# Window attention and four-expert attention on one core: stage 2 operands as two fp16 parts under a bound per batch, stage 1 softmax of four tiles at once inside PSUM

## The chip, the cores and the metric

The kernel runs on one core of one Trainium2 chip. The metric is the device time of one execution in microseconds, lower is better. The core has TensorE (PE in the rows, with its weight loads as PEld), VectorE (DVE), ScalarE (ACT), GpSimd (POOL), and SyncE (SP), which issues all the DMAs here.

## The reference

```
q, k, v: (8 batches, 8 heads, 576 positions, 64), fp32
# stage 1: sliding-window attention per head; row r sees columns r-63 .. r
scores = 0.125 * q @ k.T;  mask = (0 <= row - column < 64)
x = softmax(where(mask, scores, -1e9)) @ v        # heads side by side: x is (8, 576, 512)
# stage 2: four causal attentions ("experts") over x, the best two of them per position
logits = x @ w_gate (512, 4);  w = softmax over the top 2 of 4
for e in range(4):
    q, k, v = x @ wq[e], x @ wk[e], x @ wv[e]     # 512 -> 64
    ye = softmax(causal(0.125 * q @ k.T)) @ v @ wo[e]
    out += (weight of e in the top 2, else 0) * ye
```

wq and wk are drawn eight times larger than the other weights, so the scores of stage 2 spread widely, and operands that are rounded once are too coarse. That is why products are made of a high and a low part.

## The kernel before, in words

**Stage 1.** Two heads share a pair tile (128 partitions). One tile of work is 64 query rows of both heads against 128 key columns, the older 64 (`old`) and the block's own 64 (`own`). Four tiles are a group, so there are 72 groups `g`, nine per batch. Unit `m` (`s1_mm`, line 311) makes the scores of two groups in two PSUM banks. Unit `q` (`s1_qk`) makes the softmax: one masked minimum per tile on DVE (line 328, a custom instruction whose accumulated result is read by a second one), for groups from `FIRST` = 18 on a DVE minimum that folds the two halves into 64 columns (line 336), four exponentials on ACT, each with a read of its accumulated sum (line 339), and on POOL the division by the sum, four instructions per group (line 353). Unit `t` (`s1_t`) transposes on PE (line 376) and unfolds with masked products on DVE (line 390). Unit `a` (`s1_av`) multiplies by v (line 403) and writes x as high and low fp32r parts, `XH` on ACT (line 412) and `XL` on DVE (line 414).

**Stage 2**, for a batch `b` and a pair of experts `pr` (16 such pairs in all). Units `v` (`s2_v`) project v and the gate's logits; the product is split into three bf16 parts on ACT (line 520), DVE (line 524) and POOL (lines 527 and 528). Units `k` and `r` (`s2_k`, `s2_q`) project keys and queries into two fp32r parts, ACT for the high one and DVE for the low one; the first 64 keys and queries also go into plain fp32 tiles `KF` and `QF`. Unit `x` (`s2_mm`) makes the scores: 30 matmuls at line 625 and one fp32 product of the first block at line 628. Unit `y` (`s2_soft`) masks on DVE (line 640) and takes exponentials on ACT (line 644). Unit `u` (`s2_w`) multiplies by gate over sum and splits into two fp16 parts, the high one on ACT (line 690), the low one on POOL (lines 695 and 696) or, where `LOW` has a D and in the last three pairs, on DVE (line 693). Unit `D` transposes them by DMA (line 704). Unit `A` (`s2_av`, line 727) multiplies v by them, one pass for each entry of `PRODUCTS`; unit `o` (`s2_o`) projects with wo, ACT copies the result, and SP sends it out.

**Order.** Every unit is a generator of steps. A long string `ORDER`, written out in the file, lists the steps; each word runs one step, and a number after a colon names the PSUM banks that the unit takes (there are eight). All five engines run their instructions in the order in which the steps issue them, with semaphores between them.

## Time and profile before

| | us |
|---|---|
| median of 3 runs | 466.24 (465.84 to 468.89) |
| the profiled execution | 467.63 |
| its span, first to last instruction | 465.9 |
| busy: PE 438.8, DVE 376.6, ACT 357.2, POOL 347.3 | |

The profiled execution is 1.4 us above the median, and 1.7 us of it lie outside the span. Busy time of an engine is the union of its instructions' times. An instruction's own duration holds some time in which the next one already runs, so the spacing of starts in a run of equal instructions is the better price of one more of them.

### The profile page before, as it was taken

The numbers are of one execution on the slowest core, as the hardware profiler recorded it, in microseconds if no ns is written. First come the engines' busy times: TensorE is split into PE (matmuls) and PEld (weight loads), VectorE is DVE, ScalarE is ACT, GpSimd is POOL, SyncE is SP. The second block draws the span as 40 slices with busy tenths as digits, with TensorE's granted clock in tenths as the row PEclk, the third lists the DMA queues.
The fourth block names the chain that finished last, engine by engine and source line by source line (L and its number), as shares of the span: only waits on it lengthen the run. The fifth ranks groups of instructions, "written<-read, shape, count | busy, mean of one in ns | idle before, by whom it ended". The sixth has DMA issues, their size and how long they took to land.

```text
span 465.9 us, 17032 instructions
## 1 busy us (share of the span) xinstructions
PE 438.8 (94%) x6192; PEld 388.9 (83%) x6192; DVE 376.6 (81%) x1588; ACT 357.2 (77%) x1304; POOL 347.3 (75%) x865
## 2 busy tenths in 40 slices
PE   7898999999999999999998999999999999999955
PEld 7687899888788887888887988988898898989745
...
GB/s 261 339 275 45 36 257 220 87 156 236 98 272 229 153 171 214 129 167 215 165 163 219 201 161 182 210 136 161 245 136 168 159 146 87 134 115 183 199 183 113
DMA packets 142788, 81.86 MB, mean 176 GB/s; under 512 B 124656, under 2 KB 125680, under 8 KB 142704
## 3 DMA queue, kind: packets, MB, share of 16 engines
...
q14 instruction: 35, 0.29, 0.2%
q10 hardware_dynamic: 80, 0.13, 0.1%
...
## 4 chain that ended last, share of the span: by engine, by line
PE 21%; DVE 9%; ACT 8%; POOL 7%; DMA 4%; issue 3%; SPq 0%; DVEq 0%; POOLq 0%; ACTq 0%
PE ps L727 4%; PE ps L503 4%; DMA tu<-sp 4%; PE ps L504 3%; PE ps L505 3%; PE ps L625 3%; ACT sp L690 3%; ACT p L339 2%; PE ps L403 2%; ACT p L644 2%; POOL sp L696 2%; POOL p L353 1%; DVE sm L328 1%; DVE pt L390 1%; DVE p L336 1%
## 5 line engine op out<-in xcount | busy, mean ns | idle before, releaser
L644 ACT ACTIVATE p<-p,r 128x576 f32<-128x576 f32 (+3 forms) x128 | 77.3, 606 | 23.7 <-DVE r L640 12.1
L339 ACT ACTIVATE p<-p,st 128x64 f32<-128x64 f32 x216 | 72.3, 338 | 22.1 <-DVE p L336 21.8
L696 POOL TENSOR_TENSOR sp<-p,sp 128x320 f16<-128x320 f32 (+3 forms) x91 | 80.7, 886 | 7.6
L690 ACT ACTIVATE sp<-p,r 128x192 f16<-128x192 f32 (+3 forms) x128 | 73.1, 607 | 11.7 <-DMA tu<-sp 7.0
L390 DVE TENSOR_TENSOR pt<-ps,tri 64x512 f32<-64x512 f32 (+1 forms) x120 | 75.8, 633 | 5.0 <-PE ps L376 2.9
L353 POOL TENSOR_SCALAR p<-p,st 128x64 f32<-128x64 f32 x216 | 67.6, 336 | 5.4 <-DVE st L349 4.5
L640 DVE CUSTOM_DVE_ANT_0 p<-ps,causal 128x320 f32<-128x320 f32 (+3 forms) x160 | 68.2, 471 | 3.7 <-POOL sp L696 2.2
L727 PE MATMUL ps<-tu,v 128*64 128x64 f16 (+2 forms) x1760 | 62.1, 229 | 5.3 <-DMA tu<-sp 4.8
L727 PEld LDWEIGHTS <-v 128*64 128x64 bf16 x1760 | 59.0, 112 | 8.9 <-issue 6.7
L328 DVE CUSTOM_DVE_ANT_0 sm<-ps,win 128x128 f32<-128x128 f32 x264 | 62.3, 282 | 4.1 <-PE ps L311 3.6
L695 POOL TENSOR_SCALAR p<-p,r 128x320 f32<-128x320 f32 (+3 forms) x91 | 53.6, 589 | 5.1 <-ACT sp L690 4.2
L625 PE MATMUL ps<-kt,qt 64*128 64x320 f32 (+2 forms) x480 | 50.5, 328 | 3.1 <-DVE vr L524 1.2
L625 PEld LDWEIGHTS ps<-kt,qt 64*128 64x128 f32 x480 | 36.1, 185 | 12.6 <-DVE vr L524 1.6
L311 PE MATMUL ps<-k,q 64*64 64x128 f32 (+1 forms) x1080 | 41.4, 281 | 2.3 <-DMA k<-in_kT_dram 1.8
L403 PE MATMUL ps<-pt,v 128*64 128x64 f32 x1080 | 38.6, 225 | 3.0 <-DMA v<-in_vW_dram 1.1
L339 ACT ACTIVATION_READ_ACCUMULATOR p<-p,st 128x1 f32 x216 | 40.9, 189 | 0.0
L403 PEld LDWEIGHTS ps<-pt,v 128*64 128x64 f32 x1080 | 34.3, 138 | 6.8 <-issue 2.0
L503 PE MATMUL ps<-xh,wqhi 128*128 128x256 f32 (+1 forms) x128 | 39.4, 308 | 0.5 <-DVE vr L524 0.4
L503 PE MATMUL ps<-wvhi,xh 128*128 128x260 f32 x128 | 37.3, 292 | 2.7 <-DVE pt L390 1.9
L503 PE MATMUL ps<-xh,wkhi 128*128 128x256 f32 (+1 forms) x128 | 39.5, 309 | 0.3 <-DVE vr L524 0.2
L311 PEld LDWEIGHTS ps<-k,q 64*64 64x64 f32 x1080 | 32.0, 138 | 8.4 <-issue 3.5
L505 PE MATMUL ps<-xh,wqlo 128*128 128x256 f32 (+1 forms) x128 | 37.8, 296 | 0.0
...
## 6 DMA issues: line engine op xcount, KB each, us to landing
...
tu<-sp SPq DMA_TRANSPOSE x96, 3.7
...
```

The costliest lines, as they stand in the source:

```text
L311: nc.tensor.matmul(S1[g][i][o:o + 64, c:], lhsT=q_t[r, 64 * b:64 * b + 64], rhs=k_t[r, 64 * b + c:64 * b + 128], start=True, stop=True)
L339: nc.scalar.activation(pt[:, i], pt[:, i], AF.Exp, bias=st[:, 0, z + i:z + i + 1], scale=-1.0, accum_out=st[:, 1, z + i:z + i + 1])
L353: nc.gpsimd.tensor_scalar(p, p, st[:, 2, i:i + 1], 1.0, op0=OP.mult, op1=OP.mult)
L390: nc.vector.tensor_mul(t[64 * w:64 * w + 64, :n, e], ps[r, :n], tri[r, w, None, :].to_broadcast([64, n, 128]))
L403: nc.tensor.matmul(o[64 * h:64 * h + 64, 4 * x + i], lhsT=pairs[p][2][:, h, b], rhs=t[:, i, c:c + 64], start=True, stop=True)
L503: nc.tensor.matmul(ps, lhsT=ah, rhs=bh, start=first, stop=False)
L625: nc.tensor.matmul(ps[e][:, at(i):at(i) + n], lhsT=QT[pr][r, w, q], rhs=KT[b, pr][r, m, key:key + n], start=x == 0, stop=x == 2)
L640: nc.vector.tensor_tensor_reduce(out=dst, in0=src, in1=mask, scale=1.0, scalar=3.0e38, op0=OP.add, op1=OP.min, accum_out=to)
L644: nc.scalar.activation(p, p, AF.Exp, bias=r2[:, 0, x:x + 1], scale=-1.0, accum_out=r2[:, 1, x:x + 1])
L690: nc.scalar.activation(hi, p, AF.Copy, scale=by)
L696: nc.gpsimd.tensor_tensor(lo, p, hi, op=OP.subtract)
L727: nc.tensor.matmul(to, lhsT=V2[b % 2][:, c, a, 2 * pr + h], rhs=rhs, start=n == 0, stop=n == len(work_list) - 1, skip_group_check=True)
```

## The change

Stage 1, groups from 18 on: the scores stay in PSUM, one bank per group. One `copy_predicated` of four tiles overwrites, inside the bank, those of the `own` columns that lie in the future by the `old` ones, which leaves 64 columns per tile. Then one DVE reduction gives the four maxima. In four of nine groups (`BY_TILE`) four exponentials follow on ACT from PSUM with their sums, after POOL has scaled the maxima; in the other five DVE subtracts the maxima, ACT takes one exponential of all 256 columns, and DVE sums them. The division on POOL is one instruction per group. Where the older half doesn't exist (the first block of a head pair), a memset fills it.

Stage 2: `s1_av` also takes the largest magnitude of what it writes (`MX`). `s2_top` and `s2_scale` make three bounds per batch from it, with a matmul against the largest weights, and their reciprocals. Values, keys and queries leave PSUM multiplied by these, as two fp16 parts each. The scores are then 16-bit matmuls, the product of the first block is six 64x64 matmuls in place of the fp32 one, the product of the second block has 192 key columns in place of 256, the mask step multiplies by the product of two bounds, and `PRODUCTS` has three entries in place of five. The output copy multiplies by v's bound. All second parts are made on POOL except in the last three pairs.

`ORDER` is written anew. The diff, without it:

```diff
+FAR = 1.0e30
-LOW = "PPPPPPPDP"
+LOW = "PPPPPPPPP"
+BY_TILE = "010101010"
...
+        if i < 3:
+            nc.vector.tensor_reduce(largest[:, i:i + 1], raw, axis=AX.X, op=OP.max, apply_absolute_value=True)
+            nc.gpsimd.memset(bound[:, i], abs(scale) * 4.01 * 2.0 ** -14)
+            nc.gpsimd.tensor_scalar(bound[:, i], bound[:, i], largest[:, i:i + 1], 1.0, op0=OP.mult, op1=OP.mult)
...
     def s1_mm(gs):
+
         ps = [bank().rearrange("r (t c) -> r t c", c=128) for x in range(2)]
         for y, g in enumerate(gs):
-            S1[g] = [ps[i % 2][:, 2 * y + i // 2] for i in range(4)]
-            for i, p, b in tiles(g):
+            S1[g] = [ps[y][:, i] if len(gs) > 1 else ps[i % 2][:, i // 2] for i in range(4)]
+        for i in range(4):
+            for g in gs:
+                p, b = list(tiles(g))[i][1:]
                 c = 64 if i in alone(g) else 0
                 q_t, k_t, _ = pairs[p]
                 for h in range(2):
                     r = slice(64 * h, 64 * h + 64)
-                    o = 64 * (h ^ i % 2)
+                    o = 64 * (h ^ turn(g, i))
                     nc.tensor.matmul(S1[g][i][o:o + 64, c:], lhsT=q_t[r, 64 * b:64 * b + 64],
                                      rhs=k_t[r, 64 * b + c:64 * b + 128], start=True, stop=True)
+
+    def turn(g, i):
+        return i % 2 if g < SOLO else g % 2
...
+            old, own = (bass.AP(ps[0].tensor, ps[0].offset + 64 * x, [ps[0].ap[0], [128, 4], [1, 64]]) for x in range(2))
+            for i in lone:
+                nc.vector.memset(ps[i][:, 0:64], NEG)
+            nc.vector.copy_predicated(own, past[:, None].to_broadcast([128, 4, 64]), old)
+            yield
+            st = sums()
+            top = st[:, 0, z:z + 4]
+            if BY_TILE[g % 9] == "1":
+                nc.vector.tensor_reduce(top, own, axis=AX.X, op=OP.max, negate=True)
                 yield
-        yield
-        if g >= FIRST:
-            for x0, x1 in ((0, lone[0]), (lone[0] + 1, 4)) if lone else ((0, 4),):
-                if x0 < x1:
-                    nc.vector.tensor_tensor(pt[:, x0:x1], sm[:, x0:x1, 0], sm[:, x0:x1, 1], op=OP.min)
-            yield
-        for i in range(4):
-            nc.scalar.activation(pt[:, i], pt[:, i], AF.Exp, bias=st[:, 0, z + i:z + i + 1], scale=-1.0,
-                                 accum_out=st[:, 1, z + i:z + i + 1])
-            if i % 2:
+                nc.gpsimd.tensor_scalar(st[:, 0, z:z + 4], st[:, 0, z:z + 4], 0.125, 1.0, op0=OP.mult, op1=OP.mult)
                 yield
-        P1[g] = pt
+                pt = P1[g] = work.tile([128, 4, 64], F32, tag="p1", bufs=4, name=f"p1_{g}")
+                for i in range(4):
+                    nc.scalar.activation(pt[:, i], ps[i][:, 64:128], AF.Exp, bias=st[:, 0, z + i:z + i + 1],
+                                         scale=0.125, accum_out=st[:, 1, z + i:z + i + 1])
+                    if i % 2:
+                        yield
+                yield from normalize(g, st, z)
+                return
+            nc.vector.tensor_reduce(top, own, axis=AX.X, op=OP.max)
+            yield
+            pt = P1[g] = work.tile([128, 4, 64], F32, tag="p1", bufs=4, name=f"p1_{g}")
+            nc.vector.tensor_tensor(pt, own, top[:, :, None].to_broadcast([128, 4, 64]), op=OP.subtract)
+            yield
+            nc.scalar.activation(pt, pt, AF.Exp, scale=0.125)
+            yield
+            nc.vector.tensor_reduce(st[:, 1, z:z + 4], pt, axis=AX.X, op=OP.add)
+            yield
+        yield from normalize(g, st, z)
...
-        for i in range(n):
-            p = P1[g - (n - 1 - i) // 4][:, i % 4]
-            nc.gpsimd.tensor_scalar(p, p, st[:, 2, i:i + 1], 1.0, op0=OP.mult, op1=OP.mult)
-            if i % 4 == 3:
-                yield
+        for x in range(0, n, 4):
+            p = P1[g - 1 + x // 4 if n == 8 else g]
+            if g < FIRST:
+                for i in range(4):
+                    nc.gpsimd.tensor_scalar(p[:, i], p[:, i], st[:, 2, i:i + 1], 1.0, op0=OP.mult, op1=OP.mult)
+            else:
+                nc.gpsimd.tensor_tensor(p, p, st[:, 2, x:x + 4, None].to_broadcast([128, 4, 64]), op=OP.mult)
+            yield
...
+        if b9 not in MX:
+            MX[b9] = work.tile([128, 5], F32, tag="mx", name=f"mx_{b9}")
+        nc.vector.tensor_reduce(MX[b9][:, k // 2:k // 2 + 1], src, axis=AX.X, op=OP.max, apply_absolute_value=True)
+        yield
...
+    def s2_top(b):
+        mx, MX[b] = MX[b], work.tile([128, 1], F32, tag="top", name=f"top_{b}")
+        nc.vector.tensor_reduce(MX[b], mx, axis=AX.X, op=OP.max)
+
+    def s2_scale(b):
+        ps = bank()[:, :3]
+        top = MX.pop(b)
+        for i in range(3):
+            nc.tensor.matmul(ps[:, i:i + 1], lhsT=bound[:, i], rhs=top, start=True, stop=True)
+        yield
+
+        sc = SC[b] = work.tile([128, 7], F32, tag="sc", bufs=3, name=f"sc_{b}")
+        nc.vector.tensor_tensor(sc[:, 0:3], ps, floor, op=OP.max)
+        nc.vector.reciprocal(sc[:, 3:6], sc[:, 0:3])
+        yield
+        nc.gpsimd.tensor_tensor(sc[:, 6:7], sc[:, 1:2], sc[:, 2:3], op=OP.mult)
+        yield
+        if b % 2:
+            SC4[b] = work.tile([128, 1], F32, tag="sc4", name=f"sc4_{b}")
+            for i in range(2):
+                r = slice(64 * i, 64 * i + 64)
+                nc.gpsimd.tensor_copy(SC4[b][r], SC[b - 1 + i][r, 0:1])
...
-            dst = [V2[(b + i) % 2][at, j, a].rearrange("r e c -> r (e c)") for a in range(3)]
-            rest = work.tile([128, 256], F32, tag="vr", bufs=2, name=f"vr_{b}_{j}_{i}")[at]
-            nc.scalar.activation(dst[0], ps[r, :256], AF.Copy)
+            hi, lo = (V2[(b + i) % 2][at, j, a].rearrange("r e c -> r (e c)") for a in range(2))
+            by = SC[b + i][r, 3:4]
+            nc.scalar.activation(hi, ps[r, :256], AF.Copy, scale=by)
             yield
             if i == 0:
                 nc.vector.tensor_copy(L[b % 2][:, j], ps[:, 256:260])
-            nc.vector.tensor_sub(rest, ps[r, :256], dst[0])
-            yield
-            engine = nc.vector if b == NB - 1 else nc.gpsimd
-            engine.tensor_scalar(dst[1], rest, 1.0, 1.0, op0=OP.mult, op1=OP.mult)
-            engine.tensor_tensor(dst[2], rest, dst[1], op=OP.subtract)
-            if j == 4:
-                yield
+            nc.vector.scalar_tensor_tensor(lo, ps[r, :256], by, hi, op0=OP.mult, op1=OP.subtract)
...
+    def parts(ps, t, by):
+        nc.scalar.activation(t[:, 0], ps, AF.Copy, scale=by)
+        yield
+        nc.vector.scalar_tensor_tensor(t[:, 1], ps, by, t[:, 0], op0=OP.mult, op1=OP.subtract)
...
-    SCORES = (((1, 0, 256), (2, 0, 320)), ((3, 0, 448),), ((4, 0, 320),), ((4, 320, 256),))
+        yield from parts(ps, QT[pr][:, :, c0:c0 + n], SC[b][:, 5:6])
...
-            q = slice(128 * i - 128, 128 * i)
+            q = slice(128 * i - 64, 128 * i + 64)
...
-            nc.tensor.matmul(ps[0][:, 448:512], lhsT=QF[pr].rearrange("r a c -> r (a c)"), rhs=KF[b, pr],
-                             start=True, stop=True)
+            for x, (w, m) in enumerate(((0, 0), (0, 1), (1, 0))):
+                for e in range(2):
+                    r = slice(64 * e, 64 * e + 64)
+                    nc.tensor.matmul(ps[0][r, 448:512], lhsT=QT[pr][r, w, 0:64], rhs=KT[b, pr][r, m, 0:64],
+                                     start=x == 0, stop=x == 2)
...
+        def least(src, dst, mask, to, above=3.0e38):
+            nc.vector.tensor_tensor_reduce(out=dst, in0=src, in1=mask, scale=SC[b][:, 6:7], scalar=above,
...
-    PRODUCTS = ((0, 0), (1, 0), (2, 0), (0, 1), (1, 1))
+    PRODUCTS = ((0, 0), (1, 0), (0, 1))
...
-            copy(t[:, c], ps, h if ends else OUTS[j])
+            by = SC[b][:, 0:1] if j < 4 else SC4[b]
+            if h:
+                nc.vector.tensor_scalar(t[:, c], ps, by, None, op0=OP.mult)
+            else:
+                nc.scalar.activation(t[:, c], ps, AF.Copy, scale=by)
```

Three places show what it does to the engines' queues. VectorE, batch 4, groups 42 and 43 of stage 1 (`sm`, `p` and `st` with their numbers are the tiles of scores, exponentials and sums; `mx` holds the magnitudes for the bounds). Before:

```order
L328 ISA sm_43_3660,st_42_3631<-ps,win 128x128
L328 ISA st_42_3631 128x1
L328 ISA sm_43_3660,st_42_3631<-ps,win 128x128
L328 ISA st_42_3631 128x1
L328 ISA sm_42_3632,st_42_3631<-ps,win 128x128
L328 ISA st_42_3631 128x1
L328 ISA p_42_3633,st_42_3631<-ps,win 128x64
L328 ISA st_42_3631 128x1
L349 RECIPROCAL st_40_3386<-st_40_3386 128x8
L677 RECIPROCAL r_2_1_3363<-r_2_1_3363 128x7
L336 TENSOR_TENSOR p_42_3633<-sm_42_3632 128x192
L328 ISA sm_43_3660,st_42_3631<-ps,win 128x128
```

and in the changed kernel:

```order
L392 TENSOR_REDUCE st_42_3304<-ps 128x4
L375 COPY_PREDICATED ps<-win,ps 128x4x64
L751 RECIPROCAL r_2_0_2746<-r_2_0_2746 128x2
L395 TENSOR_TENSOR p_42_3308<-ps,st_42_3304 128x256
L751 RECIPROCAL r_2_1_3177<-r_2_1_3177 128x7
L477 TENSOR_REDUCE mx_3316<-ps 128x1
L638 TENSOR_REDUCE gs_4_3288<-gt_4_3287 128x1
L814 TENSOR_TENSOR yl_89<-ps,yh_87 128x64
L380 TENSOR_REDUCE st_42_3304<-ps 128x4
```

The per-tile rows of a group (ISA) and the fold are gone; whole-group reductions, a subtraction and the maximum of `s1_av` stand in their place.

TensorE where batch 4's stage 2 begins, the first product of v (`wvhi` by `xh`). Before:

```order
L505 MATMUL ps<-xh_3864,wklo 128x320
L503 MATMUL ps<-xh_3864,wkhi 128x320
L504 MATMUL ps<-xl_3865,wkhi 128x320
L505 MATMUL ps<-xh_3864,wklo 128x320
L503 MATMUL ps<-wvhi,xh_3864 128x260
L504 MATMUL ps<-wvlo,xh_3864 128x260
```

and in the changed kernel, with the bound's three matmuls (`bound` by `top`) ahead of it:

```order
L339 MATMUL ps<-k_3880,q_3879 64x128 x14
L339 MATMUL ps<-k_3917,q_3916 64x64 x2
L579 MATMUL ps<-top_4122,bound 128x1 x3
L567 MATMUL ps<-wvhi,xh_3314 128x260
L568 MATMUL ps<-wvlo,xh_3314 128x260
L569 MATMUL ps<-wvhi,xl_3315 128x260
```

What stood behind a product of the keys stands behind scores of stage 1 and behind the bound, which reads `top` of the same batch.

GpSimd around group 40 and 41's division (`p_40`, `p_41`), same batch. Before:

```order
L527 TENSOR_SCALAR v_1_91<-vr_0_0_3622 128x256
L528 TENSOR_TENSOR v_1_91<-vr_0_0_3622,v_1_91 128x256
L353 TENSOR_SCALAR p_40_3388<-p_40_3388,st_40_3386 128x64 x4
L496 MEMSET sp_72 128x4x64
L679 TENSOR_TENSOR r_2_1_3363<-r_2_1_3363,g_0_89 128x7
L353 TENSOR_SCALAR p_41_3392<-p_41_3392,st_40_3386 128x64 x4
L695 TENSOR_SCALAR px<-px,r_2_1_3363 128x64
L696 TENSOR_TENSOR sp_71<-px,sp_71 128x64
```

and in the changed kernel, around groups 38 and 39:

```order
L773 TENSOR_SCALAR p_1_69<-p_1_69,r_2_0_2746 128x448
L774 TENSOR_TENSOR sp_72<-p_1_69,sp_72 128x448
L417 TENSOR_TENSOR p_38_2910<-p_38_2910,st_38_2872 128x256
L749 TENSOR_SCALAR r_2_0_2746<-r_2_0_2746 128x2
L417 TENSOR_TENSOR p_39_2942<-p_39_2942,st_38_2872 128x256
L586 TENSOR_TENSOR sc_3120<-sc_3120 128x1
L623 TENSOR_TENSOR g_2_4_3240<-g_2_4_3240,below 128x16
```

The split of v (lines 527 and 528) has left this queue, the division is one instruction per group, and a product of bounds (`sc`) has come in.

## Rows read from the trace of the kernel before

**Rows 1.** The page: span, then busy time of each engine.
```profile
span 465.9 us, 17032 instructions
PE 438.8 (94%) x6192; PEld 388.9 (83%) x6192; DVE 376.6 (81%) x1588; ACT 357.2 (77%) x1304; POOL 347.3 (75%) x865
```

**Rows 2.** Windows: stretch, its length, busy us of PE, PEld, DVE, ACT, POOL, clock, DMA.
```profile
28.00:60.00 32.00, 30.48 (x353) 26.65 (x353) 22.91 (x118) 24.39 (x99) 29.32 (x80) 1.00 0.29 100
...
60.00:340.00 280.00, 269.50 (x3996) 240.48 (x3996) 252.89 (x1052) 227.54 (x864) 244.08 (x591) 1.00 0.79 183
...
140.00:180.00 40.00, 38.63 (x635) 34.27 (x634) 38.27 (x159) 32.20 (x124) 35.63 (x83) 1.00 0.85 181
...
340.00:440.00 100.00, 98.75 (x1304) 88.80 (x1300) 76.83 (x296) 74.24 (x233) 53.35 (x130) 1.00 0.78 148
...
440.00:466.00 26.00, 16.45 (x190) 13.54 (x184) 7.46 (x22) 9.52 (x21) 0.52 (x2) 0.82 0.68 152
```

**Rows 3.** Timeline of PE near 375 us: start, length, instruction, count.
```profile
373.18 2.11 PE L625 MATMUL ps<-kt,qt 64*128 64x256 f32 x24
375.22 0.43 PE L628 MATMUL ps<-kf,qf 128*128 128x64 f32 x2
375.58 1.49 PE L727 MATMUL ps<-tu,v 128*64 128x256 f16 x50
```

**Rows 4.** The chain that ended last: start, length, what.
```profile
358.25 3.65 PE ps L727 x110
```

**Rows 5.** Groups by form, weight loads: busy us, mean ns.
```profile
L727 PEld LDWEIGHTS <-v 128*64 128x64 bf16 x1760 | 59.0, 112 | 8.9 <-issue 6.7 <-DMA tu<-sp 1.0
...
L625 PEld LDWEIGHTS ps<-kt,qt 64*128 64x128 f32 x480 | 36.1, 185 | 12.6 <-DVE vr L524 1.6 <-DVE pt L390 1.5 <-issue 1.3
```

**Rows 6.** Timeline of DVE near 121 us.
```profile
121.03 0.28 DVE L328 CUSTOM_DVE_ANT_0 sm<-ps,win 128x128 f32<-128x128 f32 x1
...
121.25 0.28 DVE L328 CUSTOM_DVE_ANT_0 sm<-ps,win 128x128 f32<-128x128 f32 x1
...
121.57 0.78 DVE L336 TENSOR_TENSOR p<-sm 128x256 f32<-128x256 f32 x1
```

**Rows 7.** Groups by line on DVE: the fold.
```profile
L336 DVE TENSOR_TENSOR p<-sm 128x256 f32<-128x256 f32 (+3 forms) x66 | 32.5, 509 | 0.9
```

**Rows 8.** Groups by form on DVE: nearest rows for added and moved work.
```profile
L414 DVE TENSOR_TENSOR xl<-ps,xh 128x512 fp32r<-128x512 f32 x32 | 21.8, 686 | 1.1 <-ACT xh L412 0.7
...
L693 DVE SCALAR_TENSOR_TENSOR sp<-p,r,sp 128x576 f16<-128x576 f32 x19 | 16.2, 864 | 4.4 <-DMA tu<-sp 2.9 <-ACT sp L690 1.4
...
L524 DVE TENSOR_TENSOR vr<-ps,v 128x256 f32<-128x256 f32 x32 | 13.3, 417 | 3.9 <-POOL v L528 3.8
...
L546 DVE TENSOR_REDUCE gt<-g 128x16 f32<-128x64 f32 x8 | 1.7, 207 | 0.3 <-POOL g L542 0.3
```

**Rows 9.** Groups by line on DVE: a memset.
```profile
L250 DVE MEMSET tri<- 128x256 f32 x1 | 0.3, 272 | 0.0
```

**Rows 10.** Groups by form on ACT.
```profile
L339 ACT ACTIVATE p<-p,st 128x64 f32<-128x64 f32 x216 | 72.3, 338 | 22.1 <-DVE p L336 21.8
...
L690 ACT ACTIVATE sp<-p,r 128x320 f16<-128x320 f32 x32 | 17.2, 555 | 0.1
...
L607 ACT ACTIVATE qf<-ps 64x64 f32<-64x64 f32 x32 | 6.8, 213 | 0.2
```

**Rows 11.** Groups by form on POOL.
```profile
L353 POOL TENSOR_SCALAR p<-p,st 128x64 f32<-128x64 f32 x216 | 67.6, 336 | 5.4 <-DVE st L349 4.5
...
L528 POOL TENSOR_TENSOR v<-vr,v 128x256 bf16<-128x256 f32 x28 | 21.2, 757 | 2.3
...
L696 POOL TENSOR_TENSOR sp<-p,sp 128x576 f16<-128x576 f32 x13 | 17.6, 1352 | 1.1
...
L527 POOL TENSOR_SCALAR v<-vr 128x256 bf16<-128x256 f32 x28 | 11.5, 409 | 0.7
```

More of the change, by code (lines that the diff above doesn't have):

```diff
@@ L12 @@
 BF16 = mybir.dt.bfloat16
+U32 = mybir.dt.uint32
 AF = mybir.ActivationFunctionType
@@ L480, in clear_stage2 @@
     def clear_stage2():
-        for t in QF:
-            nc.gpsimd.memset(t, 0.0)
         nc.gpsimd.memset(below, 0.0)
@@ L791, in window_attention_moe_attention @@
     for b in range(NB):
+        unit(f"n{b}", s2_top, b)
+        unit(f"N{b}", s2_scale, b)
         for j in range(5):
```

95 lines of the change are left out of this document (48 added, 47 removed), and 264 rows, old and new, of the table ORDER.

## The prediction

> **What bounds the kernel now.** The page comes first: TensorE is busy for 94% of the span, VectorE 81%, ScalarE 77%, GpSimd 75% [rows 1]. Such shares mix stages, so the windows come next [rows 2]. Between 60 and 340 us TensorE is busy 269.5 of 280 us, and VectorE 252.9; in its densest forty, 140 to 180 us, VectorE is busy 38.27 of 40 us, as full as TensorE with 38.63. There are two bounds in this stretch, and relief of one alone gives back only what the other allows. From 340 to 440 us TensorE is busy 98.75 of 100 us and VectorE 76.8: TensorE alone bounds it. From 440 us the last pair's chain runs almost alone (TensorE 16.45 of 26 us). Ahead of 60 us TensorE and GpSimd are both over nine tenths busy (30.48 and 29.32 of 32 us). The timeline of TensorE shows that its busy time is mostly work: the rows at 373 to 376 us start where the one before is through [rows 3].
>
> The Trainium skill, "Perfetto Trace Analysis", section "Identifying the Most-Contended Engine", says that the busy share of matmuls is a poor measure, and that the share of weight loads should be read. That is 83% here beside VectorE's 81% [rows 1], which makes the two engines equal over the whole span, not in the middle alone. By this reading little of what TensorE saves would be left anywhere, and the time would be near the second rival's; by the busy shares the stretch after 340 us gives its saving back in full. The timeline, with its back-to-back rows, makes me take the second.
>
> **TensorE, part by part.** The attention product of a pair is 110 matmuls in 3.65 us [rows 4], 0.033 us each. Three products in place of five leave 66, so a pair saves 1.46 us and 16 pairs 23.4 us. The first block's fp32 product takes from 375.22 to 375.58, 0.36 us [rows 3]; six small 16-bit matmuls at 0.033 us take 0.20, so 16 pairs save 2.6 us. The scores: 24 matmuls take from 373.18 to 375.22, 0.085 us each [rows 3]. A quarter of the columns of six of them goes, 0.13 us a pair, 2 us in all. What 16-bit weights give is not in this trace. A 16-bit load of 64 columns takes 112 ns and an fp32 load of 128 takes 185 ns [rows 5], and these loads run beside matmuls, so the gain lies between nothing and the same ratio of the matmul's price: 480 times 0.085 times (1 - 112/185) is 16 us. I take 1 us, near the lower end, since the matmuls stay long. Added are 24 fp32 matmuls for the bounds, between 0.033 us [rows 4] and the 0.36 us of the first block's product [rows 3], 0.8 to 8.6 us; I take 0.25 each, 6 us, since they load the same 128 fp32 columns. Sum: -23.4 - 2.6 - 2 - 1 + 6 = **-23 us**, between -19 and -43.
>
> The Trainium skill, "TensorE: Matmul & The Clock Gate", section "Weight-path perf modes", says that weights load faster when there are 128 of them and they are not fp32. The new scores meet that, the attention product with its 64 columns does not. By it the sum would lie near -35 us; no row of this trace has such a load.
>
> **VectorE, part by part.** Removed: 192 masked minima of 128 columns, which start 0.21 us apart [rows 6], and 24 half as wide at an estimated 0.15, together 44 us; the folds, 32.5 us [rows 7]; thirteen second parts of 576 columns, moved to GpSimd, at 0.864 us [rows 8], 11 us. Together 88 us. Added: 54 `copy_predicated` of 256 elements, an operation that the trace doesn't have. The nearest row is the subtraction of 256 with one operand in PSUM and one in SBUF, 417 ns [rows 8]. The lower end is a memset of 256, 272 ns [rows 9], the upper one a fold of 256 that GpSimd's traffic drew out to 0.78 us [rows 6]. I take 0.42, as it too has one operand in SBUF: 22.5 us, with ends 15 and 42. Then 54 maxima and 30 sums of 256 elements: a reduction of 64 takes 207 ns, and an element costs 1.05 ns (686 ns for 512 against 417 for 256) [rows 8], so 0.41 us each, 34.5 us; 30 subtractions at 0.42, 12.5; the magnitudes of `s1_av`, 32 of 512 at 0.68 and 8 of 256 at 0.41, 25; 24 half memsets at 0.1, 2.5; about 5 for the small steps of the bounds, by a fifth of a us each, and 3.7 for three reductions over the weights. Together 106 us. That uses isolated lengths; in a run the next instruction starts 0.07 us before the end (0.28 long, 0.21 apart [rows 6]), which takes 14 us off the 208 long ones. Net **+4 us**, between -4 and +23. VectorE, unlike TensorE, is not relieved.
>
> **ScalarE and GpSimd.** 216 exponentials, busy 72.3 us, become 96 of 64 columns from PSUM, at 0.213 us (a copy of 64 out of PSUM) to 0.338 us (as now), and 30 of 256 at an estimated 0.50, from the 555 ns of 320 [rows 10]; with the plain fp32 copies gone ScalarE loses some 40 us. GpSimd loses 67.6 us of divisions and gets 54 of 256 with two SBUF operands at 0.757; it loses the split of v (0.409 and 0.757 us, 28 full and 8 half ones) and gets the thirteen second parts, 1.35 us each [rows 11] and some half of that again for their scaling: some 30 us less. Neither bounds the middle; their slack shortens hand-overs, for which I count nothing.
>
> **The sum, by stage.** Against the profiled execution, 467.6 us. Ahead of 60 us: nothing. GpSimd loses the first splits of v, but no key, query or value can leave PSUM before the batch's bound, which needs all nine groups; the scores of batch 1 are the cover on TensorE, and where that is not enough, a wait of some us appears. From 60 to 340 us lie 11 of the 16 pairs: TensorE would give 23 times 11/16, 16 us. VectorE has 252.9 + 3 = 256 us to do, which at its densest share (38.27 of 40) needs 267.5 us, 12.5 less than 280. The smaller counts: -12.5. From 340 us on, five pairs at 1.44 us on TensorE: -7, the last of them on the final chain. 467.6 - 19.5 = 448.1; the profiled execution lies 1.4 above the median, so **447 us**. Its own range, with the ends of the bounds' matmuls and small losses in the head, is 441 to 456.
>
> **Rivals.** *TensorE is the only bound that counts.* The middle's idle time on VectorE is then mere waiting for TensorE, and 16-bit weights are cheap: -23 to -35 us in full, so 432 to 441. For it speaks that TensorE is 96% busy in the middle and VectorE 90%; against it the windows where both are full. It is also what comes if the new weights load quickly. The Trainium skill's section on weight paths, named above, would bring that about.
>
> *VectorE is the bound everywhere in the middle.* If `copy_predicated` costs 0.78 us, VectorE has 253 + 0.7 times 23 = 269 us there, 281 us at its densest share, no gain; only the stretch from 340 us on gives 7: 461, or 456 to 466 with the reductions a little off. No change that a measurement can tell. That the change doesn't do what it says (scores in 16 bits no faster, bounds dear) ends here too.
>
> *Slower: TensorE waits for the bound, eight times.* The three small matmuls of `s2_scale` stand in TensorE's queue and wait for `top`, which follows the last magnitude of `s1_av` through VectorE's full queue; behind them stand all the projections of the batch. Price: the wait times eight. Against the 19.5 us gained it decides from 2.5 us each. With 4.5 us each, the time of some six entries in a queue at 0.7 us, 467 - 20 + 36 = 483. Against it speaks that other products can stand ahead of them in the order; for it, that the new reductions lie on just that path.
>
> **Numbers.** 447 with a chance of 0.55; TensorE alone 0.17; VectorE alone 0.18; slower 0.08; the rest, 0.02, is spread. The range 435 to 460 leaves out the far ends of the first rival, half of the second and all of the third, about 0.2. One per cent, 4.7 us, is about what a measurement of this kernel can tell: faster than 461.6 has 0.82, within one per cent 0.10, slower 0.08.
>
> **What the changed profile would show.** TensorE's attention rows 40% fewer at the same spacing, and its busy time down by some 23 us; VectorE's busy time within 15 us of 376.6 and over 95% of the middle windows; `copy_predicated` near 0.42 us; ScalarE near 315 and GpSimd near 315 busy. I am wrong if `copy_predicated` or the magnitudes take twice that, if TensorE's rows show idle time ended by `top`, or if the head grows by more than 3 us.

## The result, and the profile after

The kernel after takes **443.89 us** (443.38 to 445.15), the kernel before in the same session 467.56; the ratio is 0.950 [0.945, 0.955]. Forecast were 447, 435 to 460. The profiled execution took 443.38 us.

The page of the kernel after, the lines that answer to [rows 1]:

```profile
span 441.7 us, 15210 instructions
PE 412.7 (93%) x5600; PEld 354.6 (80%) x5600; DVE 389.7 (88%) x1312; ACT 330.2 (75%) x1046; POOL 301.4 (68%) x703
```

TensorE lost 26 us, GpSimd 46, ScalarE 27, and VectorE gained 13. The span is shorter by 24 us although VectorE has more to do.

Windows of the kernel after, columns as in [rows 2]; the 60 to 338.90 line ends at the start of the last score matmul of stage 1, the line behind it holds what follows:

```profile
28.00:60.00 32.00, 31.18 (x468) 28.12 (x466) 29.01 (x140) 27.95 (x107) 21.88 (x64) 1.00 0.47 148
60.00:338.90 278.90, 269.22 (x3790) 234.30 (x3784) 266.62 (x829) 211.62 (x668) 216.96 (x476) 1.00 0.87 191
140.00:180.00 40.00, 38.16 (x562) 32.02 (x561) 38.78 (x122) 31.41 (x99) 30.04 (x65) 1.00 0.92 211
338.90:441.70 102.80, 88.90 (x1042) 74.55 (x1036) 76.12 (x245) 72.11 (x196) 39.70 (x93) 0.96 0.77 153
```

The same two stretches of the kernel before, cut at the same instruction:

```profile
60.00:358.00 298.00, 287.16 (x4198) 255.85 (x4196) 268.11 (x1111) 241.97 (x913) 257.16 (x620) 1.00 0.79 180
358.00:465.90 107.90, 97.54 (x1288) 86.98 (x1279) 69.07 (x257) 69.34 (x203) 40.80 (x101) 0.96 0.75 153
```

This pair is the best view of the result, since the cut between its lines is the same instruction in both kernels. Their start is 60 us in both, where the kernels are not equally far: the kernel after has run 350 of the score matmuls of stage 1 by then, the kernel before 288. What I call the middle went from 298.0 to 278.9 us (-19.1), the tail from 107.9 to 102.8 (-5.1); a head cut at a fixed time can show no loss of its own. In the middle VectorE did nearly as much work, 268.1 and 266.6 us, in less time: its share rose from 90.0% to 95.6%. TensorE's share stayed, 96.4% and 96.5%.

What ended VectorE's idle time in the middle, kernel before (us in total, times, longest), the longest entries:

```profile
DVE st L349 <- POOL st L347: 4.2, 6, 1.8
DVE logits L523 <- ACT v L520: 2.9, 3, 1.8
DVE yl L736 <- ACT yh L734: 2.6, 4, 1.4
DVE p L640 <- POOL sp L696: 2.2, 3, 0.8
```

and kernel after:

```profile
DVE yl L814 <- ACT yh L812: 1.5, 1, 1.5
DVE st L399 <- ACT p L397: 1.2, 2, 1.0
DVE pt L453 <- PE ps L439: 0.9, 2, 0.6
```

Summed over the view, GpSimd ended 12.2 us of VectorE's idle time before and 0.8 after, ScalarE 9.7 and 4.2, TensorE 1.8 and 1.8. VectorE was not kept waiting by TensorE in the kernel before. It was the other way round: of the 10.3 us that TensorE waited in that stretch, VectorE ended 8.6, the longest entry being

```profile
PE ps L503 <- DVE pt L390: 1.9, 2, 1.1
```

The prices. TensorE's timeline near 222 us (answers to [rows 3]) and one entry of the chain (to [rows 4]):

```profile
222.05 1.94 PE L697 MATMUL ps<-kt,qt 64*128 64x320 f16 x24
223.92 1.18 PE L339 MATMUL ps<-k,q 64*64 64x128 f32 x32
225.12 0.83 PE L579 MATMUL ps<-top,bound 128*128 128x1 f32 x6
225.81 0.37 PE L567 MATMUL ps<-wvhi,xh 128*128 128x260 f32 x1
```
```profile
404.43 2.24 PE ps L805 x66
```

66 matmuls in 2.24 us are 0.034 each, as before. 24 score matmuls take 1.87 us to the next start, 0.078 each for 0.085; but these have 272 columns on average and those of [rows 3] had 336, so this pair says little of what 16-bit weights give. The groups by form say it at equal columns, before and then after:

```profile
L625 PE MATMUL ps<-kt,qt 64*128 64x320 f32 x192 | 21.0, 321 | 1.2 <-DVE vr L524 1.2
L625 PE MATMUL ps<-kt,qt 64*128 64x448 f32 x96 | 14.7, 386 | 0.6 <-ACT kt L593 0.3 <-DVE r L640 0.3
L697 PE MATMUL ps<-kt,qt 64*128 64x320 f16 x192 | 19.4, 298 | 0.1
L697 PE MATMUL ps<-kt,qt 64*128 64x448 f16 x96 | 12.8, 352 | 0.3 <-DVE qt L676 0.2
```

That is 8% and 13% less busy time. The three bound matmuls of a batch (six records, as an fp32 product has two) take 0.69 us, for my 0.75. Over the whole span, in the groups by line, the scores' busy time falls from 50.5 to 42.4 us, the first block's product from 7.0 to 4.5, the attention products from 62.1 to 40.0, and the bounds take 5.9.

Weight loads (to [rows 5]), then VectorE (to [rows 6 to 9]), ScalarE [rows 10] and GpSimd [rows 11], groups by form with busy us, mean ns:

```profile
L805 PEld LDWEIGHTS <-v 128*64 128x64 f16 x1056 | 36.8, 111 | 13.6 <-issue 9.7 <-DMA tu<-sp 3.4
L697 PEld LDWEIGHTS <-qt 64*128 64x128 f16 x480 | 20.2, 94 | 16.0 <-issue 8.1 <-DVE qt L676 0.9 <-DVE m L715 0.7
L375 DVE COPY_PREDICATED ps<-win,ps 128x256 f32<-128x256 uint32 x54 | 22.4, 423 | 1.4 <-PE ps L339 0.6
L477 DVE TENSOR_REDUCE mx<-ps 128x1 f32<-128x512 f32 x32 | 21.4, 675 | 0.4 <-PE ps L466 0.3
L392 DVE TENSOR_REDUCE st<-ps 128x4 f32<-128x256 f32 x30 | 12.4, 415 | 0.1
L395 DVE TENSOR_TENSOR p<-ps,st 128x256 f32<-128x256 f32 x30 | 12.2, 413 | 0.5
L715 DVE CUSTOM_DVE_ANT_0 p<-ps,causal,sc 128x320 f32<-128x320 f32 x64 | 32.4, 543 | 0.0
L611 DVE SCALAR_TENSOR_TENSOR v<-ps,sc,v 128x256 f16<-128x256 f32 x32 | 15.0, 473 | 0.0
L374 DVE MEMSET ps<- 128x64 f32 x24 | 2.7, 112 | 0.4
L386 ACT ACTIVATE p<-ps,st 128x64 f32<-128x64 f32 x96 | 28.6, 310 | 5.3 <-POOL st L382 4.5 <-POOL p L773 0.7
L397 ACT ACTIVATE p<-p 128x256 f32<-128x256 f32 x30 | 12.4, 418 | 6.1 <-DVE p L395 6.0
L607 ACT ACTIVATE v<-ps,sc 128x256 f16<-128x256 f32 x32 | 14.5, 469 | 6.5 <-PE ps L569 6.4
L417 POOL TENSOR_TENSOR p<-p,st 128x256 f32<-128x256 f32 x54 | 32.7, 613 | 6.4 <-DVE st L409 5.2 <-DVE r L751 0.4
L774 POOL TENSOR_TENSOR sp<-p,sp 128x576 f16<-128x576 f32 x26 | 33.5, 1287 | 2.2
```

The reductions and the predicated copy cost what was forecast. The masked minimum of 320 columns takes 543 ns; the kernel before, in the same groups by form, had

```profile
L640 DVE CUSTOM_DVE_ANT_0 p<-ps,causal 128x320 f32<-128x320 f32 x64 | 29.1, 485 | 2.5 <-POOL sp L696 2.2
```

The diff changed nothing in that instruction but its scale, from a constant to a column in SBUF. And the tile `top`, feared in the third rival, stopped TensorE's weight loads once:

```profile
DVE sc L583: 0.6, 2
PEld ps L579: 0.2, 1
```

### The profile page after: what moved, and what is told of

Same layout as the page of the kernel before. It is cut to its first block, busy times and chain, and to the rows that moved or that the text cites. A ratio compares the mean times of both kernels' runs of the same rounds, so it can differ in the third digit from the quotient of the medians.

```text
span 441.7 us, 15210 instructions
## 1 busy us (share of the span) xinstructions
PE 412.7 (93%) x5600; PEld 354.6 (80%) x5600; DVE 389.7 (88%) x1312; ACT 330.2 (75%) x1046; POOL 301.4 (68%) x703
## 4 chain that ended last, share of the span: by engine, by line
DVE 44%; PE 32%; POOL 6%; issue 6%; ACT 5%; DMA 5%; SPq 1%; DVEq 0%; ACTq 0%; POOLq 0%
DVE pt L453 9%; DVE p L715 9%; PE ps L567 7%; PE ps L569 6%; PE ps L568 6%; DMA tu<-sp 4%; PE ps L805 4%; DVE ps L375 3%; DVE v L611 2%; DVE xl L481 2%; DVE mx L477 2%; PE ps L466 2%; PE ps L339 2%; POOL sm L415 2%; PE ps L697 2%
## 5 line engine op out<-in xcount | busy, mean ns | idle before, releaser
L774 POOL TENSOR_TENSOR sp<-p,sp 128x576 f16<-128x576 f32 (+3 forms) x104 | 95.6, 919 | 8.7
L719 ACT ACTIVATE p<-p,r 128x192 f32<-128x192 f32 (+3 forms) x128 | 77.4, 607 | 18.2 <-DVE r L715 17.7
L715 DVE CUSTOM_DVE_ANT_0 p<-ps,causal,sc 128x320 f32<-128x320 f32 (+2 forms) x128 | 64.1, 542 | 0.2
L773 POOL TENSOR_SCALAR p<-p,r 128x576 f32<-128x576 f32 (+3 forms) x104 | 61.0, 587 | 3.4 <-ACT sp L764 2.2
L805 PEld LDWEIGHTS <-v 128*64 128x64 f16 x1056 | 36.8, 111 | 13.6 <-issue 9.7
L697 PE MATMUL ps<-kt,qt 64*128 64x320 f16 (+3 forms) x480 | 42.4, 292 | 2.1 <-DVE m L715 0.6
L567 PE MATMUL ps<-xh,wqhi 128*128 128x256 f32 (+1 forms) x128 | 39.5, 309 | 0.3 <-ACT p L386 0.3
L567 PE MATMUL ps<-xh,wkhi 128*128 128x320 f32 (+1 forms) x128 | 39.0, 305 | 0.1
L569 PE MATMUL ps<-xh,wklo 128*128 128x320 f32 (+1 forms) x128 | 37.8, 296 | 0.0
L568 PE MATMUL ps<-xl,wkhi 128*128 128x320 f32 (+1 forms) x128 | 37.8, 296 | 0.0
L568 PE MATMUL ps<-xl,wqhi 128*128 128x256 f32 (+1 forms) x128 | 37.8, 295 | 0.0
```

The costliest lines, as they stand in the source:

```text
L567: nc.tensor.matmul(ps, lhsT=ah, rhs=bh, start=first, stop=False)
L568: nc.tensor.matmul(ps, lhsT=ah, rhs=bl, start=False, stop=False)
L569: nc.tensor.matmul(ps, lhsT=al, rhs=bh, start=False, stop=last)
L715: nc.vector.tensor_tensor_reduce(out=dst, in0=src, in1=mask, scale=SC[b][:, 6:7], scalar=above, op0=OP.add, op1=OP.min, accum_out=to)
L719: nc.scalar.activation(p, p, AF.Exp, bias=r2[:, 0, x:x + 1], scale=-1.0, accum_out=r2[:, 1, x:x + 1])
L773: nc.gpsimd.tensor_scalar(p, p, by, 1.0, op0=OP.mult, op1=OP.mult)
```

## The experiments

Theory A at the start: TensorE and VectorE bind the middle together, and the time goes by their work. Rivals: TensorE's work alone (B), VectorE's alone (C), and, once these had met the first four runs, the neighbours ScalarE and GpSimd (N), and the order in which the units are called (O). All runs in one table; the time is the median, while busy us, middle and tail are those of the profiled execution, cut at the last score matmul of stage 1 as above. Each ratio is to the kernel before in the same session, which took 467.0 to 467.9 us in all of them; the kernel after was timed in the first.

| kernel | us | ratio to before | PE | DVE | ACT | POOL | middle | DVE share there | tail |
|---|---|---|---|---|---|---|---|---|---|
| before | 467.56 | 1 | 438.8 | 376.6 | 357.2 | 347.3 | 298.0 | 90.0% | 107.9 |
| after | 443.89 | 0.950 [0.945, 0.955] | 412.7 | 389.7 | 330.2 | 301.4 | 278.9 | 95.6% | 102.8 |
| before_three | 466.98 | 0.999 [0.995, 1.002] | 423.6 | 376.7 | 357.3 | 347.7 | 297.6 | 90.1% | 107.2 |
| after_five | 456.11 | 0.976 [0.973, 0.978] | 428.5 | 390.7 | 331.5 | 301.5 | 285.8 | 93.5% | 107.4 |
| bytile_none | 458.75 | 0.982 [0.979, 0.984] | 416.0 | 405.3 | 311.9 | 297.3 | 293.5 | 95.9% | 103.2 |
| no_magnitude | 440.84 | 0.940 [0.935, 0.945] | 409.0 | 370.8 | 329.6 | 301.8 | 273.5 | 92.2% | 101.5 |
| first_half | 471.88 | 1.010 [1.006, 1.013] | 438.1 | 382.4 | 306.6 | 309.2 | 303.1 | 90.4% | 107.0 |
| first_half_three | 470.92 | 1.008 [1.005, 1.011] | 424.8 | 381.8 | 306.3 | 309.0 | 304.3 | 90.0% | 106.1 |
| fold_back | 476.56 | 1.018 [1.012, 1.023] | 420.8 | 399.4 | 362.4 | 334.5 | 306.1 | 90.0% | 105.7 |
| no_pointer | 439.44 | 0.939 [0.934, 0.943] | 408.6 | 381.2 | 329.7 | 301.2 | 277.0 | 94.1% | 102.0 |
| old_order | 542.48 | 1.161 [1.157, 1.165] | 445.7 | 413.6 | 310.2 | 295.3 | 373.1 | 81.2% | 109.4 |
| divide_four | 455.77 | 0.975 [0.971, 0.978] | 417.7 | 392.1 | 330.4 | 332.3 | 289.0 | 92.9% | 104.9 |
| shared | 437.44 | 0.936 [0.932, 0.940] | 407.3 | 379.1 | 329.1 | 299.3 | 274.8 | 94.8% | 101.2 |
| no_bounds | 427.96 | 0.916 [0.912, 0.920] | 400.3 | 350.2 | 316.4 | 296.5 | 264.7 | 90.1% | 100.5 |

**before_three: the kernel before, three products.**

```diff
-    PRODUCTS = ((0, 0), (1, 0), (2, 0), (0, 1), (1, 1))
+    PRODUCTS = ((0, 0), (1, 0), (0, 1))
```

> The kernel before, with three products in place of five in the attention product of stage 2 (two passes are left out, so its output is off), all else and the order untouched: TensorE loses 23.4 us, no other engine loses anything. Theory A, two bounds in the middle: VectorE allows 12.5 us there and the end gives 7, so some 20 us less than before, 447. Rival B, TensorE alone counts: 23 us less, 443 to 444. Rival C, VectorE alone is the bound in the middle: only the stretch after 340 us gives, 7 to 8 us less, 459.

Nothing: 466.98. All theories that pay TensorE's saving miss, mine with the -7 of the tail too. Its middle, as a window:

```profile
60.00:357.60 297.60, 277.93 (x3755) 243.53 (x3754) 268.22 (x1111) 241.73 (x913) 257.29 (x619) 1.00 0.79 180
```

TensorE is relieved by 9 us there, and neither VectorE's work nor its waits move (12.2 us ended by GpSimd, 9.8 by ScalarE, 1.8 by TensorE). What TensorE saves it spends idle: 19.7 us in the middle for 10.8, and 15.1 in the tail for 10.4.

**after_five: the kernel after, TensorE's 704 matmuls put back** (two of the products done twice, which changes what is summed).

```diff
-    PRODUCTS = ((0, 0), (1, 0), (0, 1))
+    PRODUCTS = ((0, 0), (1, 0), (0, 1), (1, 0), (0, 1))
```

> The changed kernel, with two passes more in the attention product (two of the three are made twice, so its output is off): TensorE gets 23.4 us more, all else as in the changed kernel. Theory A: in the changed kernel both engines are full in the middle, so what is added to TensorE shows nearly in full: 18 to 23 us more, 462 to 467. Rival B: 23 us more, 467. Rival C: the middle hides it, 7 to 8 us more, 451.

+12.2 us, 6.9 of the profiled 11.5 in the middle and 4.6 in the tail: less than A's 18 to 23 and more than C's 7 to 8. So the same matmuls that are worth nothing in the kernel before are worth half of the gain in the kernel after.

**bytile_none: the kernel after, VectorE's work added** (maximum, subtraction and sum for all 54 groups).

```diff
-BY_TILE = "010101010"
+BY_TILE = "000000000"
```

> The changed kernel with all groups of stage 1 by whole groups (subtraction and sum on VectorE, one exponential on ScalarE): 24 groups more with 0.82 us more on VectorE, 19.7 us, some 15 us of it in the middle; ScalarE and GpSimd get less work, TensorE the same. Theory A and rival C: VectorE is a bound, so 10 to 17 us more, 454 to 461. Rival B: VectorE has slack, so within 3 us of the changed kernel, 441 to 447.

+14.9 us for 15.6 us more on VectorE and 18 us less on ScalarE; VectorE's share of the middle is at 95.9%, its highest of all runs. Here VectorE's work sets the time.

```profile
60.00:353.50 293.50, 273.77 (x3804) 236.04 (x3796) 281.37 (x876) 195.00 (x515) 213.28 (x454) 1.00 0.82 182
```

**no_magnitude: the kernel after, VectorE relieved** (the bound comes from a constant; the magnitudes are left out).

```diff
-        nc.vector.tensor_reduce(MX[b9][:, k // 2:k // 2 + 1], src, axis=AX.X, op=OP.max, apply_absolute_value=True)
+            nc.gpsimd.memset(MX[b9], 0.1)
```

> The changed kernel without the largest magnitudes of what stage 1 writes (a constant stands in for them, so the bounds are not those of the data): VectorE loses 24.7 us, and the bound no longer waits for the last of stage 1. Theory A: VectorE falls below TensorE in the middle and TensorE's 250 of 260 us stay, 4 to 12 us less, 432 to 440. Rival B: nothing, or only what the wait for the bound cost, 441 to 444. Rival C: 17 us less or more, at most 427.

-3 us for 19 us less on VectorE, between A's 432 to 440 and B's 441 to 444, so this run alone doesn't part the two. TensorE's share of the middle rises to 97.4% (in the profiled execution, 436.78 us, the shortest of its four). Together these four say: in the kernel after both engines are near their limit, in the kernel before one of them is not held by its own work.

**first_half: the kernel before with the new softmax of stage 1 alone**, in the order of before.

```diff
-            nc.vector.tensor_tensor_reduce(out=to, in0=ps[i][:, c:], in1=win[:, int(b == 0), c:], scale=-0.125, ...
...
-                    nc.vector.tensor_tensor(pt[:, x0:x1], sm[:, x0:x1, 0], sm[:, x0:x1, 1], op=OP.min)
...
+            nc.vector.copy_predicated(own, past[:, None].to_broadcast([128, 4, 64]), old)
+            nc.vector.tensor_reduce(top, own, axis=AX.X, op=OP.max)
...
+            nc.vector.tensor_tensor(pt, own, top[:, :, None].to_broadcast([128, 4, 64]), op=OP.subtract)
...
+            nc.scalar.activation(pt, pt, AF.Exp, scale=0.125)
...
+            nc.vector.tensor_reduce(st[:, 1, z:z + 4], pt, axis=AX.X, op=OP.add)
...
-                nc.gpsimd.tensor_scalar(p, p, st[:, 2, i:i + 1], 1.0, op0=OP.mult, op1=OP.mult)
+                nc.gpsimd.tensor_tensor(p, p, st[:, 2, x:x + 4, None].to_broadcast([128, 4, 64]), op=OP.mult)
```

> The kernel before with the second part of the change alone: stage 1's softmax from tile 72 on takes four tiles in one bank, folded by a predicated copy, with one exponential and one division for four (never tile by tile), in the order of before; stage 2 is as before. Worked out from rows: 54 groups x (423 + 415 + 413 + 405 ns) + 2.7 = 92 us of VectorE instead of 110 us (192 minima of 282 ns, 24 of 214 ns, 216 readings of 81 ns, 33.5 us of folds), so VectorE 377 -> 359; ScalarE 113 us -> 54 x 418 ns = 23 us, so 357 -> 267; GpSimd 67.6 -> 32.7 us, so 347 -> 312; TensorE stays at 439. Theory A (TensorE and VectorE bind together, a relief of one alone is worth nothing, TensorE can be filled to the 93% of the kernel after): 439 / 0.934 = 470, so no gain, 464 to 468. Theory N (the gain comes from the neighbours' relief, ScalarE and GpSimd and the hand-overs): 455 or less. Theory O (the gain needs the rewritten order): 467.

471.88, slower by 1% and above what any theory gave. The expectation priced the minima by their lengths (282 ns); they start 0.21 us apart [rows 6], so VectorE gained 5.8 us of work in place of losing 18. ScalarE lost 51 us and GpSimd 38, and this brought nothing: N as it stood falls.

**first_half_three: the same with three products.** The diff is that of first_half and that of before_three.

> The same kernel (order of before, stage 1's softmax of after) with three products in the weighted sums as well: it leaves out the third part of the values and one product of the rest. TensorE 439 -> 424, VectorE 359, ScalarE 267, GpSimd 312. Three products alone gave nothing (467.0). Theory A: now both bounds are lower, 424 / 0.934 = 454, so 450 to 456. Theory O (no gain without the rewritten order): 464 to 467. Theory N: the same as with the second part alone, whatever that is.

470.92, where first_half lies and far above A's 450 to 456. TensorE 14 us below before, ScalarE 51, GpSimd 38, VectorE 5 above, and the time follows VectorE's 5. A falls as a rule for any order: after_five has more work on TensorE, VectorE and ScalarE than this kernel and 8 us less on GpSimd, and is 15 us faster. The two pages, first_half_three, then after_five:

```profile
PE 424.8 (90%) x5488; PEld 370.8 (79%) x5488; DVE 381.8 (81%) x1330; ACT 306.3 (65%) x926; POOL 309.0 (66%) x703
```
```profile
PE 428.5 (95%) x6304; PEld 374.1 (83%) x6304; DVE 390.7 (86%) x1312; ACT 331.5 (73%) x1046; POOL 301.5 (67%) x703
```

**fold_back: the kernel after with the old softmax of stage 1**, in the order of after. The diff is that of first_half the other way round, with buffers enough that no tile waits for another's release in the wrong order.

> The kernel after with the second part of the change undone: stage 1's softmax by four minima, a fold of two SBUF halves, four exponentials and four divisions as before, in the order of after; stage 2 (three products, bounds) stays. VectorE 390 + 38.6 = 428 (110.2 us for 71.6), ScalarE 330 + 52 = 382, GpSimd 301 + 30 = 331, TensorE 413. Theory A: VectorE is the bound; at the 88% to 89% that it reached with 405 us (458.8), 428 us give 481 to 486, slower than before although TensorE has 23 us less. Theory O (the order carries the gain): 455 or less. Theory N: the neighbours are then where they were less GpSimd's thirds, about 460 to 467.

476.56, slower than before by 1.8% although TensorE has three products; it lies between N's 460 to 467 and A's 481 to 486, and VectorE has 399 us of work, not the 428 expected. VectorE's share of the middle is back at 90.0%, by the same kinds of wait as before; the window, then the waits:

```profile
60.00:366.10 306.10, 278.99 (x3792) 237.67 (x3784) 275.56 (x1109) 241.50 (x864) 246.36 (x599) 0.99 0.78 175
DVE logits L600 <- ACT v L597: 6.3, 7, 2.5
DVE st L402 <- POOL st L400: 6.0, 4, 2.9
DVE yl L804 <- ACT yh L802: 3.8, 4, 1.4
DVE r L741 <- POOL r L739: 3.2, 5, 1.1
```

ScalarE ends 15.2 us of VectorE's idle time and GpSimd 9.9. VectorE's own work is only 10 us above that of the kernel after, so most of the 33 us is waiting.

**divide_four: the kernel after, GpSimd's division tile by tile.**

```diff
...
-                nc.gpsimd.tensor_tensor(p, p, st[:, 2, x:x + 4, None].to_broadcast([128, 4, 64]), op=OP.mult)
+            for i in range(4):
+                nc.gpsimd.tensor_scalar(p[:, i], p[:, i], st[:, 2, x + i:x + i + 1], 1.0, op0=OP.mult, op1=OP.mult)
```

> The kernel after with one piece of stage 1 undone: GpSimd divides each tile by itself, 216 instructions of some 330 ns in place of 54 of 613 ns, so GpSimd 301 -> 337 us (76% of the span); every other engine as after. Theory A (TensorE and VectorE are the bounds): 444 to 446. Theory N (GpSimd's relief is what paid): of the 32.7 us that undoing all of stage 1's softmax cost, a third or more, 454 and up.

+11.9 us for 31 us on an engine that is 73% busy. A's 0 to 2 us is refuted, N is right here. VectorE's idle time in the middle that GpSimd ends goes from 0.8 to 5.9 us, and TensorE's waits for VectorE from 6.3 to 11. The longest entry of the former:

```profile
DVE r L748 <- POOL r L746: 2.7, 4, 1.3
```

**old_order: the work of after called in the order of before** (all groups of stage 1 by whole groups, as in bytile_none). The order of before evacuates values of a batch before its last groups of stage 1 are through, so bounds from the data have no place in it; they come from a constant.

```diff
...
-        nc.vector.tensor_reduce(MX[b9][:, k // 2:k // 2 + 1], src, axis=AX.X, op=OP.max, apply_absolute_value=True)
-        yield
+            nc.gpsimd.memset(MX[b9], 0.1)
+        idle = work.tile([128, 5], F32, tag="idle", name=f"idle_{g}")
+        nc.vector.tensor_reduce(idle[:, 0:1], src, axis=AX.X, op=OP.max, apply_absolute_value=True)
```

> The work of the kernel after, four tiles at once everywhere, but the units called in the order of the kernel before (subtraction in the step of the maximum, magnitudes in the step of the copy, weights' bounds in the step of the split). So that this order can take it, the bound of each batch comes from a constant; the 40 magnitudes are still computed, into a tile that nobody reads: the bounds from the data are left out, the work is not. To be set against the same work in the order of after, 458.75 us (by tile nowhere): TensorE 413, VectorE 405, ScalarE 312, GpSimd 301 in both. Theory W (the work of the engines sets the time, whatever the order): 456 to 461. Theory O (the order written out carries a good part of the gain): 468 or more, as the kernel before with less work on all engines but VectorE stayed at 471.

542.48. This doesn't settle O, because I put the bound's maximum and matmuls right ahead of the first product of each batch, and TensorE waits there. The waits for the tile `top`:

```profile
PEld ps L566: 26.7, 7
PE ps L566: 25.1, 7
DVE sc L570: 11.5, 8
```

Seven waits of TensorE, 3.6 us each, are the third rival as it was written; what is left, some 58 us over bytile_none, mixes what those waits delay with the order's own part. The clock may have a part in it: TensorE's granted clock is 0.93 of full speed on average in the middle, where bytile_none has 1.00, and its busy time over the whole span is 445.7 us for 416.0.

```profile
60.00:433.10 373.10, 308.33 (x3951) 262.97 (x3951) 302.80 (x931) 203.68 (x548) 219.40 (x478) 0.93 0.63 147
```

**no_pointer: the kernel after, minima with a constant scale** (the multiplication by the bounds is left out there).

```diff
-            nc.vector.tensor_tensor_reduce(out=dst, in0=src, in1=mask, scale=SC[b][:, 6:7], scalar=above,
+            nc.vector.tensor_tensor_reduce(out=dst, in0=src, in1=mask, scale=1.0, scalar=above,
```

> The kernel after with the scale of the masked minima an immediate 1.0 in place of the batch's bound in SBUF: it leaves out the multiplication by the bounds there. VectorE: 64 x 58 + 32 x 57 + 32 x 121 + 32 x 62 + 16 x 58 ns = -12.3 us if the operand in SBUF is what made these rows longer (543 against 485 ns for 320 columns), else 0. Theory A: taking 25 us of VectorE from the kernel after was worth 3, so 12 are worth 1 to 2: 441 to 443. VectorE alone as the bound: 443.9 - 12 = 432.

439.44, -4.5 us, somewhat more than A's 441 to 443 would give. The 320-column minimum is back at 483 ns:

```profile
L715 DVE CUSTOM_DVE_ANT_0 p<-ps,causal 128x320 f32<-128x320 f32 x64 | 28.5, 483 | 1.9 <-PE ps L697 1.9
```

**shared: that saving, with all of the computation kept.** Keys times 2^5 over their bound, queries times the bound over 2^5.

```diff
...
-            nc.gpsimd.memset(bound[:, i], abs(scale) * 4.01 * 2.0 ** -14)
+            nc.gpsimd.memset(bound[:, i], abs(scale) * 4.01 * 2.0 ** (-5 if i == 1 else -14))
...
-        yield from parts(ps, QT[pr][:, :, c0:c0 + n], SC[b][:, 5:6])
+        yield from parts(ps, QT[pr][:, :, c0:c0 + n], SC[b][:, 1:2])
...
-            nc.vector.tensor_tensor_reduce(out=dst, in0=src, in1=mask, scale=SC[b][:, 6:7], scalar=above,
+            nc.vector.tensor_tensor_reduce(out=dst, in0=src, in1=mask, scale=1.0, scalar=above,
```

> A version meant to beat both: keys are multiplied by 2^5 over the keys' bound and queries by the bound over 2^5, so that their product needs no scale. The masked minima have the immediate scale 1.0, the queries' own bound, its matmul and its weight maximum go. The output is the reference's. VectorE 390 -> 376 (12.3 us of minima, 1.2 us of a maximum), the rest as after. From the run without the pointer (439.4): 438 to 440. If that run owed its gain to its wrong exponents: 444.

**437.44**, 6.4 us below the kernel after: it beats both, so no_pointer's gain does not hang on the factor that its result lacks.

**no_bounds: two fp16 parts with no bounds at all** (the guard against numbers beyond fp16 is left out).

```diff
...
-        nc.vector.tensor_reduce(MX[b9][:, k // 2:k // 2 + 1], src, axis=AX.X, op=OP.max, apply_absolute_value=True)
...
-            nc.vector.scalar_tensor_tensor(lo, ps[r, :256], by, hi, op0=OP.mult, op1=OP.subtract)
+            nc.vector.tensor_sub(lo, ps[r, :256], hi)
...
-            nc.vector.tensor_tensor_reduce(out=dst, in0=src, in1=mask, scale=SC[b][:, 6:7], scalar=above,
+            nc.vector.tensor_tensor_reduce(out=dst, in0=src, in1=mask, scale=1.0, scalar=above,
```

> The kernel after with values, keys and queries as two fp16 parts without any bound: no magnitudes (24.7 us), no scale in the minima (12.3), plain subtractions for the second parts (104 x 58 ns = 6), no bounds (4), so VectorE 390 -> 343 and ScalarE 330 -> 317; TensorE 413 -> 409. It leaves out the guard against numbers that fp16 cannot hold. Theory A (TensorE binds as soon as VectorE is relieved, in an order fitted to more work on VectorE): TensorE's share stays at 93% to 94%, 435 to 440. VectorE alone as the bound: 400.

427.96, lower than A's 435: 39.5 us less on VectorE, 14 on ScalarE and 12 on TensorE give 16. Its middle:

```profile
60.00:324.70 264.70, 258.79 (x3699) 226.16 (x3699) 238.42 (x772) 198.49 (x651) 212.84 (x458) 1.00 0.91 198
```

TensorE is 97.8% busy and VectorE 90.1%, which points to TensorE as the bound; no run relieved it here. The bounds cost 16 us of what the change could give.

## Why the prediction was right, and where not

The time was right, and so was the mechanism for the kernel after: in its middle VectorE does 266.6 us of work at 95.6%, and the sum had put it at its densest share of before, 38.27 of 40 or 95.7% [rows 2]. bytile_none ended at 95.9%. The terms:

- **TensorE -23**, measured -26.1. By their own rows the products gave 22.1 of my 23.4, the first block 2.5 of 2.6, and the bounds took 5.9 of 6; mis-sized were the scores, 8.1 for 3. (In before_three and after_five the whole engine's busy time moved by 15 to 16 us only, as other rows grew or shrank.) The Trainium skill, "TensorE: Matmul & The Clock Gate", section "Weight-path perf modes", says that loads of 128 16-bit weights run about twice as fast. The trace agrees: 128 of them load in 94 ns, where 64 take 111 and the 128 fp32 ones took 185 [rows 5]. The scores gained 5 us more than I took. By that rule I had put the sum at -35, 12 us beyond mine and without a working; the other 7 did not come. Nor did the reading by the share of weight loads hold, which put the time near the second rival.
- **VectorE +4**, measured +13.1, inside the bounds of -4 to +23. Mis-sized was a term that I did not have: a scale read from SBUF. The minima of 320, 448 and 192 columns are 57 to 62 ns longer, those of 256, with two such operands, 121 (61 with one, in no_pointer), and the second parts of values, keys and queries some 56 to 63. By the rows' lengths that is 18 us; no_pointer took 8.5 us off VectorE's busy time.
- **ScalarE -40**, measured -27, for the same reason: copies of 256 columns take 469 ns for 377, of 512 columns 685 for 590. The Trainium skill, "ScalarE: Activation LUTs", section "What ACT_TABLE_LOAD costs", gives about 93 ns for each such operand. The trace agrees, with 92 and 95; in no_bounds, which has no such operand, the same copies take 375 and 594.
- **GpSimd -30**, measured -46. The forecast did not add up its own rows: 67.6 us of divisions and some 41 of splits off, 40.9 of divisions and some 26 of second parts on, come to about -42. The division took 613 ns for my 757, 8 us more.
- **Head, nothing**: right, as far as a cut at 60 us shows it. TensorE is 31.18 of 32 us busy there, as the cover needed.
- **Middle, -12.5**: measured -19.1, with the end at 358 us of the kernel before and not at 340. Of VectorE's 13 us none lay in the middle (268.1 to 266.6); 7.6 went into the first 60 us and 7 into the tail, where it had room. 266.6 at 95.7% is 278.6, and 278.9 was measured.
- **Tail, -7 on TensorE in full**: measured -5.1, and after_five gives 4.6 of it back. Of the attention products six pairs lie behind 340 us in the kernel before (660 of 1760 matmuls), not the five that the sum took.

The step that failed is the reading of the kernel before. The prediction said that from 340 us on "TensorE alone bounds it" and that in the middle "relief of one alone gives back only what the other allows". before_three relieved TensorE alone, by 5.4 us in the tail and 9.2 in the middle, and the tail gave 0.7 us, the middle 0.4. VectorE at 90% was not at a limit of its own in the middle, and it was not waiting for TensorE either: its waits were for ScalarE and GpSimd. And of these the prediction said "their slack shortens hand-overs, for which I count nothing". fold_back and divide_four price them, 33 and 12 us. The densest forty microseconds gave the right ceiling, and the change happened to remove what kept the kernel under it. That VectorE came up to 95.6% is thus not owed to TensorE's relief alone, as the sum had it, and that the time fits to 3 us is in part luck.

Rivals. TensorE alone falls with before_three, no_magnitude's 97.4% notwithstanding; VectorE alone falls with after_five, and its dear `copy_predicated` was 423 ns; the wait for `top` cost 0.2 us of loads, with scores of stage 1 ahead of it in the queue, and old_order shows its price where the bound stands right ahead of the products that need it.

**Open.** Why the shorter hand-overs of first_half bring nothing in the order of before, while taking them away costs 33 us in the order of after. In first_half_three VectorE waits less for GpSimd (12.2 to 4.9 us) and more for TensorE (1.8 to 6.8), and its share stays at 90.0%. That the order, written for the times of one kernel, turns each relief into a wait somewhere else fits all runs but is not shown by any; the one run that was to show it, old_order, is spoilt by its own wait for the bound. A new order for the old work was not tried.
